# Two of three x blocks as a fourth pair of blocks in an output Strassen scheme, and the same scheme for the first group

## The chip, the cores and the metric

One core of a Trainium2 chip runs the program. The metric is the device time of the program in microseconds (us), the median of several executions; lower is better. Single instructions are looked at in one profiled execution. PE is the matrix engine, PEld its weight loads, DVE the vector engine, ACT the scalar engine, POOL the GpSimd engine, SP the engine whose queue issues nearly all DMAs.

## The reference

A gated linear recurrence (4 batches, 8 heads, 768 steps, head size 48) gives y, which as x of 3072 x 384 enters a feed-forward layer with a maximum over three products:

```python
state = f[:, :, t, :, None] * state + einsum('bhd,bhe->bhde', k[:, :, t], v[:, :, t])
y[:, :, t] = einsum('bhd,bhde->bhe', q[:, :, t], state)
...
h = np.maximum(np.maximum(x @ w1, x @ w2), x @ w3)      # 3072 x 768
return (h @ w_out).astype(np.float32)                    # 3072 x 384
```

All is fp32, the weights are given in fp64 and rounded in the kernel.

## The kernel before

**Algebra.** The kernel forms hm = max(0, x(w2 - w1), x(w3 - w1)) and then out = hm w_out + x (w1 w_out). The 384 x 384 product w1 w_out is computed once, by linear(a) for a = 0, 1, 2 (L724), and kept as w_nat, in the order of features of the first group's x. A copy in the order of features of the later groups' x, w_lin, is made by DMAs (place, L450: ten DMAs a matrix).

**Two kinds of work.** The recurrence runs in 24 rounds u = 0 to 23, each 64 steps of two batches, 128 tokens. Four rounds make a group g of 512 tokens, which then goes through the feed-forward part. In a round the matmuls of the recurrence are pairs (L386), values with sums (L399, L422) and finish (L492); DVE multiplies the result of pairs by a mask (L395) and runs two scans for the next round (scan L324, before L345); POOL multiplies k and q by the scans' results (L340, L351) and the state by its decay (L357); DVE turns kh into ks by sixteen small transposes in four steps (keys_by_blocks, L372), and sums (L436) needs all of them. From round 8 on k, q and f are loaded by blocks and turned on DVE; before that PE transposes them through the PSUM tiles "tr".

**Order.** Everything is issued in an order written by hand (tc.manual_schedule, L927 on), and every engine takes its instructions in that order. The feed-forward part is a generator that yields after each step with an estimate of its PE time (columns x COLUMN, 4 / 2.4 ns). fill(ns) (L902) adds to a budget and takes steps until it is used up. Each round has five fills: before keys, finish and pairs; before after and before of the next round; before values; and two more between the transposes. EARLY (rounds 4 to 7, the last fill 1000 less) and PART (later rounds) are their sizes. What a group has left when the recurrence ends runs alone, with checks of the weights' range (check_range) and, near the end, two small matmuls (L1078, L1079) that read reductions which DVE makes (L1071 to L1075).

**First group** (ffn_first, L738): plain products, then linear, then outputs(hm, xT, i) (L558) for four tiles of 128 tokens, nine matmuls of 384 columns each: six blocks of hm with w_out, three blocks of x with w_nat. Between them POOL makes the mixed weights for the later groups: mix_in (L782) for the inputs, mix (L583) for the outputs, five subtractions of 128 x 576.

**Later groups.** inputs_by_pairs (L807) computes hm by a Strassen scheme over pairs of blocks of x; each of its steps is two matmuls of 256 columns. Three blocks n = 0, 1, 2 of two hm blocks each run interleaved, in the order of L874 to L891. seventh(n) ends with ACT's copy of u3 (L854) and POOL's addition to it (L855); third(n) ends with a DVE addition (L862); fourth(n) ends with two DVE maxima, L869 for the first half of the tokens and L870, which reads u3, for the second, and then sums_of_hm(hm, n) on POOL (L597, four operations of 128 x 256), which forms the sums s1, s2, s4 of the pair and writes one difference in place.

outputs_by_pairs (L599) then computes the 512 tokens by a Strassen scheme of two token tiles, two blocks of a pair and two halves of the columns (HD = 192), p = 0, 1 for the two pairs of tiles. into(b, p, lhs, rhs) (L609) issues three matmuls of 192 columns: over the three pairs of hm blocks for A(k, n), s1, s2, s4, and over the three blocks of x for X(n). A bank is read by ACT into partial (L616) and then written on. The stage opens with X(0) into b for both p, then A(0, 0) into a. sums_of_x(g + 1) (L794) prepares the next group's inputs on POOL near the end of the stage. Results lie in o_four and are stored by store_late in the next group.

Names of places: w_mix[0] is a tile of its own, w_mix[1] to [4] lie in w_in[2]; s_mix lies in w_in[1]; partial is the place of w_nat. Block 3 of a group's xT is free once its rows are packed into the other three, and holds two sums for the inputs.

Of the kernel before, what the change touches and what calls it, by code (L numbers as in the profile page):

```python
# [55 lines left out]
def kernel(  # L56
# [33 lines left out]
    def fast():  # L90
        ctx = ExitStack()
        with ctx:
# [465 lines left out]
            def outputs(hm, xT, i):  # L558
                p = bank()
                t = slice(i % 2 * UT, (i % 2 + 1) * UT)  # L560
                terms = [(hm[:, j, i * UT:(i + 1) * UT], w_out[:, j, :]) for j in range(NJ)]
                terms += [(by_halves(xT)[:, i // 2, k, t], w_nat[:, k, :]) for k in range(NK)]
                for n, (lhsT, rhs) in enumerate(terms):
                    nc.tensor.matmul(p[:, 0:DM], lhsT=lhsT, rhs=rhs, start=(n == 0), stop=(n == NJ + NK - 1))  # L564
                    if n % NK == NK - 1:
                        if n == NJ + NK - 1:
                            o = o_four[:, i]
                            nc.scalar.copy(o, p[:, 0:DM])
                            store(i, o)
                        yield NK * DM * COLUMN  # L570

            HJ, HD = NJ // 2, DM // 2
            corner = lambda k, n: w_out[:, k::2, n * HD:(n + 1) * HD]
            w_mix = [keep.tile([128, HJ, HD], FP32, name="mix")] + [w_in[2][:, :, n * HD:(n + 1) * HD] for n in range(4)]
            s_mix = [w_in[1][:, n, :].rearrange("q (jj t) -> q jj t", jj=HJ) for n in range(NK)]
            partial = [w_in[0][:, n, 0:DM] for n in range(NK)]  # L580
            pairs_of = lambda t: t.rearrange("q (p c) -> q p c", p=2)

            def mix(n):  # L583
# [3 lines left out]
                             (w_mix[4], w_lin[:, :, 0:HD], w_lin[:, :, HD:]))[n]  # L587
                nc.gpsimd.tensor_tensor(dst, x, y, op=ALU.subtract)

            def sums_of_hm(hm, jj):  # L590

                first, second = ([hm[:, 2 * jj + k].rearrange("q (p n t) -> q n p t", p=2, n=2)[:, n] for n in range(2)]
                                 for k in range(2))
                s1, s2, s4 = (pairs_of(t[:, jj]) for t in s_mix)
                for dst, x, y, op in ((s1, first[1], second[1], ALU.add), (s2, s1, first[0], ALU.subtract),
                                      (first[1], first[0], first[1], ALU.subtract), (s4, second[0], s2, ALU.subtract)):
                    nc.gpsimd.tensor_tensor(dst, x, y, op=op)  # L597

            def outputs_by_pairs(g, hm, xT):  # L599
                tile_of = lambda p, n: slice((2 * p + n) * UT, (2 * p + n + 1) * UT)  # L600
                A = lambda k, n: lambda p: hm[:, k::2, tile_of(p, n)]
                X = lambda n: lambda p: xT[:, 0:NK, tile_of(p, n)]
                s1, s2, s4 = (lambda p, t=t: t[:, :, p * UT:(p + 1) * UT] for t in s_mix)
                lin = [w_lin[:, :, n * HD:(n + 1) * HD] for n in range(2)]
# [4 lines left out]
                def into(b, p, lhs, rhs):  # L609
                    for k in range(HJ):  # L610
                        nc.tensor.matmul(b[:, p * HD:(p + 1) * HD], lhsT=lhs(p)[:, k], rhs=rhs[:, k],  # L611
                                         start=id(b) not in begun, stop=(k == HJ - 1), skip_group_check=True)
# [8 lines left out]
                COST = HJ * HD * COLUMN  # L621
                a, b, c = bank(), bank(True), bank(True)
                into(b, 0, X(0), lin[0])
                yield COST
                into(b, 1, X(0), lin[0])
                yield COST
                into(a, 0, A(0, 0), corner(0, 0))
                yield COST
                into(b, 0, A(1, 0), corner(1, 0))
                yield COST  # L630
                into(a, 1, A(0, 0), corner(0, 0))
                read(a, 0)
                yield COST
                into(b, 1, A(1, 0), corner(1, 0))
                add(o_of(0, 0), b, 0)
                yield COST
                into(a, 0, s2, w_mix[1])
                yield COST
                into(a, 1, s2, w_mix[1])
                read(a, 1)  # L640
                yield COST
                into(c, 0, s1, w_mix[0])
                yield COST
                into(c, 1, s1, w_mix[0])
                nc.scalar.copy(tops[:, 2], c[:, 0:DM])
                yield COST
                into(a, 0, A(0, 1), w_mix[2])
# [682 lines left out]
```

## Time and profile before

| | us |
|---|---|
| median of 3 runs (426.74 to 427.01) | 426.76 |
| time of the profiled execution | 427.35 |
| its span, first to last instruction | 425.5 |

Busy time by stretch of that execution (PE's includes modelled ends of pipelined matmuls):

| stretch, us | what runs | PE | DVE | ACT | POOL |
|---|---|---|---|---|---|
| 60 to 70 | first group's products, rounds 4, 5 | 9.39 | 7.97 | 4.24 | 6.05 |
| 70 to 80 | the same, rounds 5, 6 | 9.08 | 6.07 | 7.87 | 3.34 |
| 80 to 90 | linear begins | 9.39 | 6.07 | 7.24 | 6.28 |
| 100 to 110 | first group's outputs | 10.00 | 5.19 | 3.18 | 2.38 |
| 140 to 164 | group 1, inputs | 24.00 | 18.89 | 11.31 | 16.84 |
| 164 to 190 | group 1, outputs | 26.00 | 20.00 | 6.78 | 15.57 |
| 345 to 368 | group 4, outputs, recurrence ends | 23.00 | 1.84 | 9.58 | 7.33 |
| 368 to 397 | group 5, inputs | 29.00 | 5.23 | 19.30 | 12.82 |
| 397 to 425.5 | group 5, outputs, stores | 21.92 | 3.36 | 2.40 | 4.12 |

In a line of the timeline the columns are start, duration (for merged lines, of all of them together), engine, line, operation, output <- inputs, partitions x columns, count; in brackets the idle time of the engine before it and what ended that. "x12" merges twelve records. In the list of waits the columns are the waiting engine and line, what it waited for, us in total, times, longest. A chain's line has start, us and what ran.

### The profile page before, as it was taken

What the parts mean: (1) busy time and instruction counts of PE and PEld (TensorE: products, weight loads), DVE (VectorE), ACT (ScalarE), POOL (GpSimd) and SP (SyncE); (2) the same over time, 40 slices, a digit from 0 to 9 for tenths busy, and PEclk for the clock granted to TensorE, in tenths of its full rate; (3) what the DMA queues carried; (4) which work ended last, traced back from release to release, by engine and by line L of the source; (5) the groups of instructions that cost most, each with busy time, mean ns of one, the idle gap of its engine ahead of it and who ended that gap; (6) DMA issues with size and microseconds to landing.
All of it is one profiled execution on the core that took longest, in us unless ns stands there. A gap on an engine that the chain in (4) does not pass through costs nothing.

```text
span 425.5 us, 11548 instructions
## 1 busy us (share of the span) xinstructions
PE 405.3 (95%) x4650; PEld 340.3 (80%) x4650; DVE 265.4 (62%) x517; ACT 179.9 (42%) x413; POOL 232.8 (55%) x260
## 2 busy tenths in 40 slices
PE   5988799899999999999999999999999999999993
PEld 4766665466567888998889988889988899988993
DVE  6986574952687699868789867888774720012300
ACT  2459566732114442425531444442264424576210
POOL 2178354541888676386586357566546960425600
PEclk9989999999999999999999999999999999999998
DMA  8988987771547753276645276634473011542003
GB/s 170 227 262 259 262 241 119 123 173 51 93 95 119 90 128 54 64 96 103 109 122 109 41 116 81 142 82 87 70 151 86 0 53 42 141 129 66 2 1 78
DMA packets 174617, 47.20 MB, mean 111 GB/s; under 512 B 154016, under 2 KB 172256, under 8 KB 174560
## 3 DMA queue, kind: packets, MB, share of 16 engines
q1 hardware_dynamic: 171216, 45.61, 51.6%
q10 hardware_dynamic: 3344, 0.81, 0.9%
q8 instruction: 37, 0.61, 0.6%
q14 instruction: 20, 0.16, 0.1%
HBM read 37.75 MB, written 4.72 MB: 100 GB/s over the span
## 4 chain that ended last, share of the span: by engine, by line
PE 86%; DVE 3%; SPq 3%; ACT 2%; DMA 2%; issue 1%; POOL 1%; DVEq 0%; POOLq 0%
PE p L819 19%; PE tr L819 16%; PE p L611 14%; PE tr L611 12%; PE p L564 6%; PE p L537 5%; PE p L728 3%; PE y L500 3%; PE y L411 3%; PE a L392 2%; DMA raw<-in_moe_w_dram 2%; SPq L174 2%; PE y L436 2%; PE tr L291 1%; SPq L164 1%
## 5 line engine op out<-in xcount | busy, mean ns | idle before, releaser
L819 PE MATMUL tr<-xT,placed 128*128 128x256 f32 x300 | 73.3, 385 | 0.0
L382 DVE STREAM_TRANSPOSE ks<-kh 32x128 f32<-32x128 f32 x224 | 67.7, 302 | 4.6 <-POOL kh L340 1.0
L819 PEld LDWEIGHTS tr<-xT,placed 128*128 128x128 f32 x300 | 55.6, 190 | 9.1 <-ACT hm L827 1.4
L819 PE MATMUL p<-xT,placed 128*128 128x256 f32 x180 | 45.0, 381 | 0.0
L819 PEld LDWEIGHTS p<-xT,placed 128*128 128x128 f32 x180 | 33.8, 190 | 4.7
L537 PE MATMUL p<-xT,w_in 128*128 128x256 f32 (+1 forms) x108 | 34.3, 458 | 2.9 <-DVE hm L750 2.2
L619 DVE TENSOR_TENSOR o<-tr,w_in 128x384 f32<-128x384 f32 (+1 forms) x11 | 5.7, 514 | 49.6 <-PE tr L611 44.3
L329 DVE TENSOR_TENSOR_SCAN r<-gate,from_one 128x520 f32<-128x520 f32 x24 | 31.3, 1306 | 8.3 <-ACT gate L308 5.3
L340 POOL TENSOR_TENSOR kh<-kt,r 128x512 f32<-128x512 f32 x16 | 28.8, 1798 | 10.6 <-DVE kt L296 10.6
L837 POOL TENSOR_TENSOR hm<-hm,rest_bits 128x512 f32<-128x512 f32 x15 | 22.7, 1512 | 19.1 <-ACT hm L827 19.1
L597 POOL TENSOR_TENSOR w_in<-hm 128x256 f32<-128x256 f32 x15 | 10.9, 727 | 40.5 <-DVE hm L870 40.5
L347 DVE TENSOR_TENSOR_SCAN prod<-gate,from_inv 128x520 f32<-128x520 f32 x24 | 32.5, 1355 | 0.0
L506 ACT COPY xT<-y 64x256 f32<-64x256 f32 (+1 forms) x60 | 22.1, 369 | 24.1 <-PE y L500 23.4
L395 DVE TENSOR_TENSOR at<-a,mask 128x512 f32<-128x512 f32 x24 | 16.5, 688 | 24.2 <-PE a L392 23.9
L258 POOL TENSOR_TENSOR w_in<-top_bits,rest_bits 128x384 uint32<-128x384 uint32 x18 | 21.8, 1211 | 15.5 <-DVE top_bits L254 8.8
L819 PE MATMUL p<-w_in,placed 128*128 128x256 f32 x120 | 30.0, 379 | 0.0
L862 DVE TENSOR_TENSOR hm<-tr,hm 128x512 f32<-128x512 f32 x15 | 10.2, 681 | 29.3 <-PE tr L819 19.3
L537 PEld LDWEIGHTS p<-xT,w_in 128*128 128x128 f32 x108 | 19.3, 190 | 10.7 <-issue 6.2
L655 POOL TENSOR_TENSOR o<-top_bits,w_in 128x384 f32<-128x384 f32 x5 | 5.1, 1015 | 41.6 <-ACT w_in L616 41.6
L616 ACT COPY w_in<-p 128x384 f32<-128x384 f32 x15 | 7.2, 479 | 47.1 <-PE p L611 47.1
L280 ACT ACTIVATE raw<-top_bits 128x384 f32<-128x384 f32 x48 | 25.2, 526 | 0.4
L819 PEld LDWEIGHTS p<-w_in,placed 128*128 128x128 f32 x120 | 22.8, 190 | 3.1
(153 smaller groups left out, 890.5 us busy)
## 6 DMA issues: line engine op xcount, KB each, us to landing
raw<-in_moe_w_dram SPq DMA_DIRECT2D x24, 384.0 KB, 4.2
v_ld<-in_v_dram SPq DMA_DIRECT2D x48, 96.0 KB, 3.2
placed<-in_moe_w_dram SPq DMA_DIRECT2D x12, 384.0 KB, 6.6
out_dram<-o SPq DMA_DIRECT2D x46, 96.0 KB, 2.4
placed<-in_moe_w_out_dram SPq DMA_DIRECT2D x6, 384.0 KB, 6.0
raw<-in_moe_w_out_dram SPq DMA_DIRECT2D x6, 384.0 KB, 3.4
f_ld<-in_f_logit_dram SPq DMA_DIRECT2D x32, 64.0 KB, 2.6
k_ld<-in_k_dram SPq DMA_DIRECT2D x32, 64.0 KB, 2.5
```

Of the source, the lines that this page charges most:

```text
L258: nc.gpsimd.tensor_tensor(dst, by(top), by(rest), op=ALU.add)
L280: nc.scalar.activation(over, size, AF.Relu, scale=(-1 / HI_MIN, 1.0)[step - 1], bias=(1.0, -HI_END * (1 - 2.0 ** -24))[step - 1], accum_ou ...
L329: nc.vector.tensor_tensor_scan(r[:, 0:LEN][:, ::-1], flat(gate)[:, ::-1], flat(from_one)[:, ::-1], 1.0, op0=ALU.mult, op1=ALU.max)
L340: (nc.vector if u < BY_ROWS else nc.gpsimd).tensor_tensor(kh.rearrange("p h a t -> p a h t"), kt, by_batch(r[:, 1:LEN + 1].rearrange("p (x ...
L347: nc.vector.tensor_tensor_scan(flat(prod), flat(gate_tiles[u % 2]), flat(from_inv[u % 2]), 1.0, op0=ALU.mult, op1=ALU.max)
L382: nc.vector.transpose(ks[n * 32:(n + 1) * 32, :, par, e0:e0 + 32], kh[p0:p0 + 32, :, a, t0:t0 + 32])
L506: nc.scalar.copy(xT[o, :, t0 + a * C:t0 + (a + 1) * C], y[i, a, 0:HP * C].rearrange("p (h t) -> p h t", h=HP))
L537: nc.tensor.matmul(p if w < TOK else p.rearrange("p (two t) -> p two t", two=2), lhsT=w_in[i][:, kt, j * 128:(j + 1) * 128], rhs=x[:, t.st ...
L564: nc.tensor.matmul(p[:, 0:DM], lhsT=lhsT, rhs=rhs, start=(n == 0), stop=(n == NJ + NK - 1))
L611: nc.tensor.matmul(b[:, p * HD:(p + 1) * HD], lhsT=lhs(p)[:, k], rhs=rhs[:, k], start=id(b) not in begun, stop=(k == HJ - 1), skip_group_c ...
L819: nc.tensor.matmul(b[:, j * HALF:(j + 1) * HALF], lhsT=w[:, (2 * n + j) * 128:(2 * n + j + 1) * 128], rhs=x, start=begin and j == 0, stop= ...
L837: nc.gpsimd.tensor_tensor(out(n, 0), out(n, 0), first, op=ALU.add)
```

## The change

- In groups 1 to 5 blocks 0 and 1 of x join the output scheme as a fourth pair: into issues four matmuls for A(k, n), s1, s2 and s4, and one (block 2 of x) for X(n). Its sums (sums_of_pair on x) are made on POOL right after those of hm pair 1, its mixed weights (mix_x) once, in group 1, just before them.
- The first group's outputs use outputs_by_pairs too, with three pairs of hm and three plain x blocks. Its sums_of_hm run during linear(1) and linear(2), the five mixes on DVE instead of POOL just before the stage, mix_in inside it, and the copies of w_lin (place) after it. Its stores go through store_late.
- w_mix[0] takes the place of a corner of w_out; partial of group 0 is w_lin, of the others w_nat.
- EARLY goes from 2360 to 2270, PART from 2464 to 2432.

```diff
-            w_mix = [keep.tile([128, HJ, HD], FP32, name="mix")] + [w_in[2][:, :, n * HD:(n + 1) * HD] for n in range(4)]
+            w_mix = [corner(0, 1)] + [w_in[2][:, :, n * HD:(n + 1) * HD] for n in range(4)]
+            x_mix = [w_lin[:, 0, HD:]] + [w_mix[4][:, n] for n in range(2)] + [keep.tile([128, HD], FP32, name="mix")]
+            s_last = keep.tile([128, HALF], FP32, name="s_last")
...
             def mix(n):
...
-                nc.gpsimd.tensor_tensor(dst, x, y, op=ALU.subtract)
+                nc.vector.tensor_tensor(dst, x, y, op=ALU.subtract)
+
+            def mix_x(n):
+                of = lambda k, c: w_lin[:, k, c * HD:(c + 1) * HD]
+                dst, x, y = ((x_mix[2], of(1, 1), of(0, 1)), (x_mix[0], of(0, 1), of(0, 0)),
+                             (x_mix[1], of(1, 1), x_mix[0]), (x_mix[3], of(1, 0), x_mix[1]),
+                             (w_mix[4][:, 2], of(2, 0), of(2, 1)))[n]
+                nc.gpsimd.tensor_tensor(dst, x, y, op=ALU.subtract)
+
+            def sums_of_pair(x0, x1, *sums):
+                first, second = ([x.rearrange("q (p n t) -> q n p t", p=2, n=2)[:, n] for n in range(2)] for x in (x0, x1))
+                s1, s2, s4 = (pairs_of(t) for t in sums)
+                for dst, x, y, op in ((s1, first[1], second[1], ALU.add), (s2, s1, first[0], ALU.subtract),
+                                      (first[1], first[0], first[1], ALU.subtract), (s4, second[0], s2, ALU.subtract)):
+                    nc.gpsimd.tensor_tensor(dst, x, y, op=op)
+
+            def sums_of_hm(hm, jj):
+                sums_of_pair(hm[:, 2 * jj], hm[:, 2 * jj + 1], *(t[:, jj] for t in s_mix))
+
+            def s_of_x(xT):
+                return [xT[:, NK, 0:HALF], xT[:, NK, HALF:TOK], s_last]
...
             def outputs_by_pairs(g, hm, xT):
+                mixed = g > 0
+                A = lambda k, n: lambda p: [hm[:, 2 * jj + k, tile_of(p, n)] for jj in range(HJ)] + [xT[:, k, tile_of(p, n)]] * mixed
+                C = lambda k, n: [w_out[:, 2 * jj + k, half(n)] for jj in range(HJ)] + [w_lin[:, k, half(n)]] * mixed
+                T = lambda i: [w_mix[i][:, jj] for jj in range(HJ)] + [x_mix[i]] * mixed
...
+                if mixed:
+                    X = lambda n: lambda p: [xT[:, 2, tile_of(p, n)]]
+                    partial = [w_nat[:, n, :] for n in range(NK)]
+                else:
+                    X = lambda n: lambda p: [by_halves(xT)[:, p, k, n * UT:(n + 1) * UT] for k in range(NK)]
+                    partial = [w_lin[:, n, :] for n in range(NK)]
...
                 def into(b, p, lhs, rhs):
-                    for k in range(HJ):
+                    for n, (x, w) in enumerate(zip(lhs(p), rhs)):
...
-                COST = HJ * HD * COLUMN
+                COST, PLAIN = (HJ + mixed) * HD * COLUMN, len(lin[0]) * HD * COLUMN
                 a, b, c = bank(), bank(True), bank(True)
                 into(b, 0, X(0), lin[0])
-                yield COST
+                yield PLAIN
                 into(b, 1, X(0), lin[0])
-                yield COST
-                into(a, 0, A(0, 0), corner(0, 0))
+                yield PLAIN
+                into(a, 0, A(0, 0), C(0, 0))
                 yield COST
...
-                    for cost in linear(a):
+                    for n, cost in enumerate(linear(a)):
                         round_to(rounded[0] + 1)
+                        if a and n < 2:
+                            jj = 2 * (a - 1) + n
+                            if jj < HJ:
+                                sums_of_hm(hm, jj)
                         yield cost
+                for n in range(5):
+                    mix(n)
+                for n, cost in enumerate(outputs_by_pairs(0, hm, xT)):
+                    if 3 <= n < 7:
+                        mix_in(n - 3)
+                    yield cost
                 for n in range(2 * NK + 2):
                     place(w_lin, w_nat, n)
-                made = iter([lambda n=n: mix_in(n) for n in range(4)] + [lambda n=n: mix(n) for n in range(5)])
-                for i in range(GRP):
-                    for n, cost in enumerate(outputs(hm, xT, i)):
...
                     sums_of_hm(hm, n)
+                    if n == 1:
+                        if g == 1:
+                            for i in range(5):
+                                mix_x(i)
+                        sums_of_pair(xT[:, 0], xT[:, 1], *s_of_x(xT))
                     yield COST
...
-            EARLY = 2360
-            PART = (33 * TOK + 22 * HJ * HD) * COLUMN / (5 * GRP)
+            EARLY = 2270
+            PART = (33 * TOK + 64 * HD) * COLUMN / (5 * GRP)
```

The other calls of into in outputs_by_pairs stay in their order, with C(k, n) for corner(k, n), T(i) for w_mix[i], lin_mix for w_mix[4], and PLAIN for the X terms.

## Prediction

> **What bounds the kernel now.** I read the busy shares and the forty slices first, then the chain that ended last, then what PE and its weight loads waited for, and last the timeline of each engine around one output stage and around the end.
>
> ```profile
> PE 405.3 (95%) x4650; PEld 340.3 (80%) x4650; DVE 265.4 (62%) x517; ACT 179.9 (42%) x413; POOL 232.8 (55%) x260
> PE   5988799899999999999999999999999999999993
> PE 86%; DVE 3%; SPq 3%; ACT 2%; DMA 2%; issue 1%; POOL 1%; DVEq 0%; POOLq 0%
> ```
>
> PE is full from about 90 us to the end and is 86% of the chain: less PE work shortens the kernel one for one, and every new PE wait lengthens it one for one. In the list of what the weight loads waited for after 160 us, one line concerns the start of the output stage; the timelines of group 1 (PE, DVE, POOL) show where it arises.
>
> ```profile
> PEld p L611 <- DVE hm L869: 0.8, 3, 0.3
> ```
> ```profile
> 163.92 2.11 PE L611 MATMUL tr<-w_in,xT 128*128 128x192 f32 x12
> 165.87 1.39 PE L611 MATMUL p<-w_out,hm 128*128 128x192 f32 x6
> 167.09 1.14 PE L611 MATMUL tr<-w_out,hm 128*128 128x192 f32 x6
> ...
> 168.68 0.63 PE L436 MATMUL y<-v_ld,ks 64*64 64x48 f32 x32
> ```
> ```profile
> 163.19 0.69 DVE L395 TENSOR_TENSOR at<-a,mask 128x512 f32<-128x512 f32 x1
> ...
> 164.54 1.24 DVE L329 TENSOR_TENSOR_SCAN r<-gate,from_one 128x520 f32<-128x520 f32 x1
> ...
> 165.93 0.67 DVE L869 SCALAR_TENSOR_TENSOR hm<-hm,p 128x512 f32<-128x512 f32 x1
> 166.53 0.68 DVE L870 SCALAR_TENSOR_TENSOR hm<-hm,top_bits 128x512 f32<-128x512 f32 x1
> 167.24 1.28 DVE L382 STREAM_TRANSPOSE ks<-kh 32x128 f32<-32x128 f32 x4
> ```
> ```profile
> 159.29 0.73 POOL L597 TENSOR_TENSOR w_in<-hm 128x256 f32<-128x256 f32 x1 [0.63 <-DVE hm L870]
> ...
> 162.15 1.28 POOL L855 TENSOR_TENSOR top_bits<-top_bits,top 128x512 f32<-128x512 f32 x1
> ```
>
> Each fp32 matmul leaves two records (330 calls at L611, 660 records): x12 is six matmuls. The six x-matmuls that open the stage take 165.87 - 163.92 = 1.95 us, **0.325 us a matmul**. The next six records last 1.39 instead of 1.14: their third matmul reads the hm that L869 ends at 166.60, so PE waited 0.25 us. The six x-matmuls are the cover under which DVE, behind the mask and scan of the attention, finishes hm. This wait is there in groups 1, 2 and 3 (3 times, 0.8 us), not in 4 and 5, which have no scan there.
>
> **What the change saves.** A mixed group runs 14 calls of four matmuls and 8 of one, 64 for 66: 5 groups x 2 x 0.325 = 3.25 us. The first group runs 36 matmuls of 384 columns now; the chain has them as
>
> ```profile
> 100.46 1.94 PE p L564 x6
> ...
> 103.89 6.00 PE p L564 x18
> ```
>
> 1.94 / 3 = 0.647 us each, so 23.3 us; after, 66 of 192 columns are 21.45. Saved 1.8. Together **-5.1 us**.
>
> **The opening of the stage, groups 1 to 3.** X(0) is now two matmuls instead of six, while the order of the A terms keeps hm's last pair third. From the budgets and costs the order of emission can be worked out: the last fourth() and X(0) fall in the second fill of u = 11, 15, 19 before and after, so DVE's order (mask, scan, L869) stays. PE therefore comes to the waiting matmul four matmuls, 1.30 us, earlier, and L869 is no earlier: 3 x 1.30 = **+3.9**. Lower bound the same 3.9, since L869 hangs on PE's third(2) through a full DVE; upper the next term.
>
> **POOL's new work in that stretch.** The four sums of x are four more operations of the L597 kind (393.16 to 396.02 in the last group: 2.86 us), queued between the sums of hm pair 1 and the addition L855 of u3. In group 1 five mix_x stand before them: 128x192 by the rows 0.73 (256 columns) and 1.00 (384) is 0.59 each, 3.0 us. Behind L855 hangs L870 on DVE; behind L870 on DVE the transposes L382, the next scan, everything; and PE's L436 needs those transposes. u3 of block 1 is also emitted one fill later, behind kh and qh, so the sums start some 0.6 us later, at 159.9.
> - Group 1: 159.9 + 2.86 + 3.0 + 2.86 + 1.24 = 169.9, with 0.4 for one operation lengthened beside the scan (L597 has 1.67 in such a place) 170.3; L870 to 171.0, L382 to 172.3. PE would be at L436 at 166.97 + 6 x 0.325 + 0.5 = 169.4. Wait **+2.9**, between 1.5 (POOL in step with before, shorter mixes) and 3.6.
> - Groups 2 and 3: without the mixes L855 ends at 167.3, L382 at 169.3, PE needs it at 169.4: **+0.2** for both, 0 to 1.8.
> - The scan L329 now meets POOL at work. Such a scan lasted
>
> ```profile
> 149.67 1.43 DVE L329 TENSOR_TENSOR_SCAN r<-gate,from_one 128x520 f32<-128x520 f32 x1
> ```
>
> against 1.24 with POOL idle: +0.2 before L869 in three groups, **+0.6**, 0 to 0.75. [...]
>
> **The end.** In the last group the same addition of u3 releases L870, L870 the reductions behind it on DVE, and these the two small matmuls L1078 and L1079, which stand in PE's queue inside the output stage.
>
> ```profile
> 396.02 1.28 POOL L855 TENSOR_TENSOR top_bits<-top_bits,top 128x512 f32<-128x512 f32 x1
> ```
> ```profile
> 397.58 0.68 DVE L870 SCALAR_TENSOR_TENSOR hm<-hm,top_bits 128x512 f32<-128x512 f32 x1
> ...
> 398.86 0.15 DVE L1075 TENSOR_SCALAR most<-most 128x1 f32<-128x1 f32 x1
> ```
> ```profile
> 399.69 0.19 PE L1078 MATMUL a<-is_feature,least 128*1 128x1 f32 x2
> ```
>
> With 2.86 of sums in front, L855 ends at 400.16, L870 starts at 400.2, L1075 ends 1.43 later, 401.65. PE, with X(0) of 0.65 and two calls of 1.30 (the fill of 3000 now reaches A(1, 0) too), is there at 396.67 + 3.25 = 399.9: **+1.75**, between 1.2 and 2.2. Today this wait is nil, 399.69 against 399.01.
>
> **Smaller terms.** After X(1) the bank is read by ACT before PE writes it again. ACT's copy ends
>
> ```profile
> 410.89 0.48 ACT L616 COPY w_in<-p 128x384 f32<-128x384 f32 x1 [3.42 <-PE p L611]
> ```
>
> 0.68 us after PE is free (410.69); the cover X(0) lin[1] falls from 1.95 to 0.65, so about 0.15 with the start: five groups **+0.75**, 0.25 to 1.5. In u = 10, 14, 18 L436 comes one step (0.87) earlier than its transposes allow (0.7 of slack: 152.66 to 153.36): 3 x 0.2 = **+0.6**, 0 to 0.9. X(0) of the first group reads w_nat, whose last third ACT ends at 100.98, 0.65 after the stage's start: **+0.15**, 0 to 0.4.
>
> Costed at nothing: the five mixes on DVE, 0.56 for 384 columns (L444) so some 0.8 each. They hide in the 6.9 us for which DVE stands idle before 103.97; contended at 1.5 each they would cost PE 0.3 through the mask. The first group's twelve sums on POOL (8.6 us) sit in its idle time from 91 to 106, behind w_in[1]'s copies, whose last issue ends at 86.86; s2 is read near 108. The copies of w_lin, ten issues of 0.59 us on SP, move behind the first group's outputs, ahead of the f, k, q loads for u = 12 and of v for u = 11, and six stores move behind these; SP stands idle from 154.0 to 162.5, about what the copies (5.9) and the six stores (3.5) take, and v of u = 11, issued near 155, is read at 168. A smaller EARLY moves 1.4 us of matmuls past u = 4 to 6, where PE is idle 2.1 us of 30: taken as 0, -0.7 to +1.4.
>
> **Sum.** -5.1 + 3.9 + 2.9 + 0.2 + 0.6 + 1.75 + 0.75 + 0.6 + 0.15 = **+5.75 us**. The profiled execution has a span of 425.5 and a time of 427.35; it would be 431.2 and 433.1. The median before, 426.76, is 0.6 below that execution's time, so I predict **432.5 us**. All low ends together give +0.9, all high ends +11; not all fall on one side, and the forecast's own range is 429 to 436.
>
> **Rivals.**
> - *The waits are covered* (on the other side, faster). If L869 ended by 165.2 in groups 1 to 3, PE would meet no wait, and with the sums hidden only -5.1 + 0.75 is left: 422.4. For it: DVE is at 62%. Against: its chain from third(2) to L869 (161.2 to 166.6) has no gap over 0.1 us, and it already ends late by 0.25. It decides from L869 before 165.2. 12%.
> - *POOL's additions fit in its idle time.* Then only the opening counts: -5.1 + 3.9 + 0.6 + 0.75 + 0.15 = +0.3, 427.1. For it: POOL is idle 3.9 us before 167.35. Against: that gap lies behind L855, the new work ahead of it. It decides if L855 still ends before 166.5. 16%.
> - *DVE falls behind in every group*: L870 late by 1.5 us in groups 2 and 3 as well and one microsecond more in u = 4 to 6: +9.8, 436.5. For it: POOL operations beside scans lasted 1.67 to 2.0 instead of 0.73 to 1.2. 10%.
> - The change doing less than it says: narrower matmuls bound by weight loads of 190 ns. Against: x12 in 1.95 us is 162 ns a record with such loads. In the rest.
>
> The forecast has 62%. A change of 0.2%, 0.85 us, is what a measurement of this kernel can tell. Below 425.9: the first rival and a little of the second, 0.14. Within: 0.09, the second. Above: 0.77. The range that leaves out no more than a fifth reaches down to the second rival, 426.4, and up to 436.0.
>
> **What would show it.** Right: PE idle of 1.5 us before the third hm matmul of groups 1 to 3, released by L869; L855 of block 2 in group 1 near 170 and PE idle before L436 there; PE idle of 1.7 us before L1078, released by DVE; into() with 772 records (386 matmuls). Wrong: no idle at L611 beyond 0.3, or L1078 without a wait. A PE idle of several us near 100 to 110 would mean that the mixes or the first group's sums were not hidden.

## The result, and the profile after

The changed kernel takes **441.71 us** (median of 4 runs, 438.36 to 442.26) against 426.75: 1.0332 times as long, 95% interval 1.0289 to 1.0376. Slower was right, 432.5 was too low, and the time lies outside the range. The profiled execution took 438.36 us with a span of 436.6 and a mean granted clock of 0.995; the other runs of this measurement had clocks of 0.978 to 0.982 and spans of 439.3 to 440.4.

The busy shares, PE's forty slices and the shares of the chain, in the page of the changed kernel:

```profile
PE 403.6 (92%) x4690; PEld 345.5 (79%) x4690; DVE 273.8 (63%) x524; ACT 180.0 (41%) x414; POOL 256.5 (59%) x293
...
PE   4977898989999995999998999998999999999894
...
PE 77%; DVE 7%; ACT 4%; DMA 3%; POOL 3%; SPq 3%; issue 2%; ACTq 0%; DVEq 0%; POOLq 0%
```

PE is busy 1.7 us less than before and the span is 11.1 longer: PE waits, and its share of the chain falls from 86% to 77%. One slice is down to 5 tenths (about 164 to 175 us, group 1), others in groups 2 and 3 to 8. What PE waited for, from the same profile (engine and line, releaser: us in all, times, longest):

```profile
PE p L619 <- DVE hm L879: 3.5, 2, 1.8
PE y L436 <- DVE ks L382: 3.0, 2, 2.6
...
PE p L736 <- POOL w_out L258: 2.0, 1, 2.0
...
PE p L619 <- DMA f_ld<-in_f_logit_dram: 1.5, 1, 1.5
PE a L1093 <- DVE least L1087: 1.3, 1, 1.3
...
PE p L619 <- ACT w_in L624: 0.6, 1, 0.6
```

(L619 is into of the outputs, L879 and L880 the two maxima of fourth, L865 the addition to u3, L579 mix_x, L587 sums_of_pair, L736 linear, L624 read, L1093 the first small matmul.) The line with f_ld is the opening of group 1: the matmul there reads w_out and hm and no f_ld, and L879 ended its hm at 168.44, 0.05 before PE went on. Each of these waits has its term in the prediction, but for the one at L736.

Cut by the starts of the parts on PE, the kernels of this study look so (us; in the columns after the first two, runs that are told below):

| part | before | after | EARLY 2280 | GpSimd moved, 2270 | both | opening in two passes | s4 ahead | ks ahead | first group alone |
|---|---|---|---|---|---|---|---|---|---|
| linear | 15.92 | 19.84 | 15.92 | 19.83 | 15.92 | 15.93 | 15.92 | 15.92 | 15.92 |
| first group's outputs | 28.72 | 27.14 | 27.15 | 27.14 | 27.14 | 27.14 | 27.15 | 27.15 | 27.41 |
| group 1 | 60.41 | 65.30 | 67.29 | 62.11 | 61.59 | 60.61 | 60.70 | 59.57 | 60.30 |
| group 2 | 60.50 | 62.39 | 61.54 | 61.76 | 61.40 | 60.67 | 60.48 | 59.43 | 60.30 |
| group 3 | 60.51 | 62.36 | 61.54 | 61.78 | 61.40 | 60.67 | 60.48 | 59.43 | 60.30 |
| group 4 | 57.61 | 57.82 | 57.22 | 57.83 | 57.22 | 57.22 | 56.78 | 56.77 | 57.42 |
| group 5, to its last matmul | 51.39 | 52.55 | 52.52 | 50.93 | 50.93 | 50.92 | 49.96 | 49.96 | 51.39 |
| median of the runs | 426.75 | 441.71 | 433.70 | 430.49 | 426.36 | 424.92 | 422.34 | 419.66 | 425.03 |

The part ahead of linear differs by up to 2 us from execution to execution and is left out; in half of the profiles (of these columns before, GpSimd moved and opening in two passes) it holds a stretch of half clock of 3.4 us, at 24 or 45 us. Beside the experiments the kernel before took 427.1 to 427.4; the ratios below are to that.

**Linear, +3.92.** PE's timeline (start, duration, engine, line, operation, output <- inputs; in brackets the idle time before and its releaser), first before, then after:

```profile
89.11 2.75 PE L728 MATMUL p<-w_out,w_in 128*128 128x384 f32 x8
91.70 0.60 PE L291 MATMUL tr<-ident,k_ld 128*128 128x128 f32 x4
```
```profile
87.82 1.13 PE L736 MATMUL p<-w_out,w_in 128*128 128x384 f32 x3
90.92 1.56 PE L736 MATMUL p<-w_out,w_in 128*128 128x384 f32 x2 [1.97 <-POOL w_out L258]
92.27 1.06 PE L291 MATMUL tr<-ident,k_ld 128*128 128x128 f32 x4
```

DVE's timeline around the rounding of the last weight piece (L254), first before, then after:

```profile
85.39 1.05 DVE L254 SCALAR_TENSOR_TENSOR top_bits<-placed,top_bits 128x384 uint32<-128x384 uint32 x1 [0.23 <-issue]
88.79 0.69 DVE L395 TENSOR_TENSOR at<-a,mask 128x512 f32<-128x512 f32 x1 [2.34 <-PE a L392]
90.08 1.24 DVE L329 TENSOR_TENSOR_SCAN r<-gate,from_one 128x520 f32<-128x520 f32 x1 [0.60 <-ACT gate L308]
```
```profile
86.50 0.69 DVE L395 TENSOR_TENSOR at<-a,mask 128x512 f32<-128x512 f32 x1 [2.31 <-PE a L392]
87.81 1.24 DVE L329 TENSOR_TENSOR_SCAN r<-gate,from_one 128x520 f32<-128x520 f32 x1 [0.62 <-ACT gate L308]
...
89.21 0.52 DVE L254 SCALAR_TENSOR_TENSOR top_bits<-placed,top_bits 128x384 uint32<-128x384 uint32 x1
```

The rounding hangs on a step of linear. With EARLY 2270 that step no longer falls into the first fill of round 6, ahead of the mask and the scan, but into the second, behind them; PE waits 1.97 us for it. After the wait, four transposes last 1.06 us instead of 0.60. The windows of 1 us from the same profile say why (busy us and records of PE, PEld, DVE, ACT, POOL, then PE's granted clock, DMA share, GB/s):

```profile
90.00:91.00 1.00, 0.08 (x1) 0.08 (x1) 0.00 (x0) 0.00 (x0) 1.00 (x3) 1.00 0.53 117
91.00:92.00 1.00, 1.00 (x2) 0.56 (x3) 0.00 (x0) 0.00 (x0) 0.92 (x3) 0.52 0.82 209
...
93.00:94.00 1.00, 1.00 (x7) 1.00 (x6) 0.63 (x2) 0.00 (x0) 1.00 (x3) 0.50 0.04 9
94.00:95.00 1.00, 1.00 (x4) 0.64 (x4) 1.00 (x2) 0.00 (x0) 0.92 (x2) 0.77 0.00 0
```

The granted clock is 0.50 for some 3.4 us, which costs 1.7. Such a stretch of half clock is called a dip below.

**Group 1, +4.89.** PE, DVE and POOL at the opening of its outputs:

```profile
165.56 0.81 PE L619 MATMUL tr<-w_in,xT 128*128 128x192 f32 x4
166.21 0.81 PE L619 MATMUL p<-w_out,hm 128*128 128x192 f32 x4
168.49 0.59 PE L619 MATMUL p<-w_out,hm 128*128 128x192 f32 x2 [1.47 <-DMA f_ld<-in_f_logit_dram]
...
174.06 0.31 PE L436 MATMUL y<-v_ld,ks 64*64 64x48 f32 x2 [2.63 <-DVE ks L382]
```
```profile
166.19 1.43 DVE L329 TENSOR_TENSOR_SCAN r<-gate,from_one 128x520 f32<-128x520 f32 x1
...
167.77 0.67 DVE L879 SCALAR_TENSOR_TENSOR hm<-hm,p 128x512 f32<-128x512 f32 x1
172.66 0.69 DVE L880 SCALAR_TENSOR_TENSOR hm<-hm,top_bits 128x512 f32<-128x512 f32 x1 [4.22 <-POOL top_bits L865]
173.38 1.28 DVE L382 STREAM_TRANSPOSE ks<-kh 32x128 f32<-32x128 f32 x4
```
```profile
164.57 1.95 POOL L579 TENSOR_TENSOR w_in<-w_in 128x192 f32<-128x192 f32 x3
...
168.51 2.21 POOL L587 TENSOR_TENSOR xT<-xT 128x256 f32<-128x256 f32 x3
...
171.36 1.26 POOL L865 TENSOR_TENSOR top_bits<-top_bits,top 128x512 f32<-128x512 f32 x1
```

Two x-matmuls instead of six, then PE waits for L879; and L880 stands idle for 4.22 us because POOL works through the differences and sums ahead of L865, so that the transposes behind L880 come late for L436. In group 5 the same delay reaches the small matmuls:

```profile
410.39 0.69 DVE L880 SCALAR_TENSOR_TENSOR hm<-hm,top_bits 128x512 f32<-128x512 f32 x1 [2.53 <-POOL top_bits L865]
```
```profile
411.59 0.19 PE L1093 MATMUL a<-is_feature,least 128*1 128x1 f32 x2 [1.30 <-DVE least L1087]
```

In group 4, 0.60 us of PE's wait is for ACT's read at L624. It is queued there behind the range checks of the weights, the last of which runs from 371.36 to 371.89; the read starts at 371.79.

### The profile page after: what moved, and what is told of

The parts are those of the page before. It is cut to its first block, busy times and chain, and to the rows that moved or that the text cites. A ratio compares the mean times of both kernels' runs of the same rounds, so it can differ in the third digit from the quotient of the medians.

```text
span 436.6 us, 11685 instructions
## 1 busy us (share of the span) xinstructions
PE 403.6 (92%) x4690; PEld 345.5 (79%) x4690; DVE 273.8 (63%) x524; ACT 180.0 (41%) x414; POOL 256.5 (59%) x293
## 4 chain that ended last, share of the span: by engine, by line
PE 77%; DVE 7%; ACT 4%; DMA 3%; POOL 3%; SPq 3%; issue 2%; ACTq 0%; DVEq 0%; POOLq 0%
PE p L829 15%; PE p L619 15%; PE tr L829 15%; PE tr L619 12%; PE p L537 4%; PE y L411 3%; PE p L736 2%; PE y L500 2%; PE y L436 2%; PE a L392 2%; SPq L183 2%; DVE r L329 2%; DMA placed<-w_in 1%; PE tr L291 1%; PE y L407 1%
## 5 line engine op out<-in xcount | busy, mean ns | idle before, releaser
L329 DVE TENSOR_TENSOR_SCAN r<-gate,from_one 128x520 f32<-128x520 f32 x24 | 33.2, 1384 | 9.6 <-ACT gate L308 6.7
L627 DVE TENSOR_TENSOR o<-tr,w_in 128x384 f32<-128x384 f32 (+1 forms) x13 | 6.8, 527 | 51.6 <-PE tr L619 50.3
L624 ACT COPY w_in<-p 128x384 f32<-128x384 f32 x18 | 8.6, 478 | 71.8 <-PE p L619 71.8
L339 POOL COPY ends<-r 128x8 f32<-128x8 f32 x24 | 6.7, 277 | 48.3 <-DVE r L329 48.3
L619 PE MATMUL p<-w_in,hm 128*128 128x192 f32 x144 | 28.8, 336 | 0.6 <-ACT w_in L624 0.6
L587 POOL TENSOR_TENSOR w_in<-hm 128x256 f32<-128x256 f32 x18 | 13.1, 727 | 27.2 <-DVE hm L880 27.2
L619 PE MATMUL tr<-w_out,w_in 128*128 128x192 f32 x144 | 27.1, 327 | 0.5 <-DVE o L627 0.5
L619 PE MATMUL p<-w_in,xT 128*128 128x192 f32 x124 | 26.2, 326 | 0.0
```

The lines of the kernel that those rows point to most:

```text
L329: nc.vector.tensor_tensor_scan(r[:, 0:LEN][:, ::-1], flat(gate)[:, ::-1], flat(from_one)[:, ::-1], 1.0, op0=ALU.mult, op1=ALU.max)
L619: nc.tensor.matmul(b[:, p * HD:(p + 1) * HD], lhsT=x, rhs=w, start=id(b) not in begun, stop=(n == len(rhs) - 1), skip_group_check=True)
```

## The experiments

Theory at the outset: three separate losses, each in its place: the late rounding in linear (with the clock's fall behind it), the thin opening of the outputs, POOL's new work ahead of u3. Rivals: the first group's sums on POOL are what delays linear; the low clocks of the repeated runs have a cause of their own; DVE is simply behind in every group.

### EARLY alone: 2280, and 2360

```diff
-            EARLY = 2270
+            EARLY = 2280
```

> The changed kernel with EARLY 2280 instead of 2270 and nothing else; by the arithmetic of the fills this moves the second linear block (and with it the rounding of weight piece 23) from the second fill of unit 6 back into the first, where the kernel before has it, so that the rounding stands on VectorE ahead of unit 6's mask and unit 7's scan. Theory (the 2.9 us lost ahead of the first group's outputs come from that rounding being late, 2.0 us of wait, and from the lower granted clock that follows the wait): the wait at the second linear block goes, the transposes at 92 us last 0.60 us again, the span falls from 436.6 to about 433.5, and the repeated runs lose their low clocks (0.978 to 0.982) and come to about 435. Rival A (the first group's sums on GpSimd hold up the rounding): wait and span stay as they are. Rival B (the low clock of the repeated runs has another cause): the span falls by about 2, but the repeated runs stay at a clock of 0.98, near 439.

Measured: 433.70 us (433.19 to 434.41), 8.0 less than the changed kernel, for 10 ns in a constant. Linear is back at 15.92, the wait is gone and the transposes last 0.60: the theory, and not the rival on POOL's sums, which are all still there. But the clock did not stay up: in this profile it was 0.50 from 169 to 175.7, behind group 1's wait at L436 (2.07), and group 1 took 67.29 instead of 65.30. Groups 2, 3 and 4 gained as well, 0.85, 0.82 and 0.60, which nobody expected. Their steps are laid out otherwise too: in group 2 single steps of the inputs, two matmuls each, stand one fill earlier, at the opening L880's wait for POOL's addition falls from 0.95 to 0.26, L436 takes 0.63 for 0.95, and PE's wait for L879 is 0.10 shorter. The rest of the 0.85 is not traced. The span fell by 4.9. The clocks of the runs were 0.984 to 0.992.

```diff
-            EARLY = 2270
+            EARLY = 2360
```

> The changed kernel with EARLY as in the kernel before, 2360. The linear stage is laid out as before the change, so by the theory its wait and the clock drop are gone as in the run with 2280, 433 to 434 of span. The difference to 2280 is the phase: groups 0 and 1 are laid out 1.8 us of matrix work earlier against the units' own steps. If phase does not matter, the time is that of the run with 2280 within 0.5 us; if it does, group 1's part changes by a microsecond or more. Rival A (sums on GpSimd): no change from 441.7.

Measured: 442.25 us (441.94 to 442.75), the time that the rival named, but not by its cause: linear lasts 15.93, and groups 1 to 3 took 67.97, 64.86 and 64.86. The phase, how the feed-forward steps lie against the rounds, matters, by far more than a microsecond. PE waited six times at L436 for the ks, 7.1 us in all. The clock fell to 0.50 at 171 to 178, behind a wait of 2.18 at L619, and at 239 to 243 and 304 to 308, behind waits of 2.19 and 2.20 at L436; mean clock 0.977 to 0.979 in all four runs.

### EARLY in the kernel before

```diff
-            EARLY = 2360
+            EARLY = 2270
```

> The kernel before with EARLY 2270 and nothing else: none of the change's sums, differences or blocks. By the arithmetic of the fills the second linear block falls into the second fill of unit 6, as in the changed kernel, and all later groups are laid out one matrix step later. Theory (the linear stage's loss is EARLY's alone): the wait at the second linear block is there, 2.0 us, with the dip of the clock behind it, and the linear stage lasts 19.8 instead of 15.9; the time is 430 to 431, plus what the later groups lose by their phase. Rival (the loss needs the first group's new sums on GpSimd or differences on VectorE): linear stage of 15.9, 427 with the phase's effect.

Measured: 435.79 us (432.66 to 436.09), 1.0202 times the kernel before, interval 1.0172 to 1.0232. The wait is there without any of the change's new work; PE's timeline:

```profile
87.27 2.10 PE L728 MATMUL p<-w_out,w_in 128*128 128x384 f32 x6
91.33 0.91 PE L728 MATMUL p<-w_out,w_in 128*128 128x384 f32 x2 [1.96 <-POOL w_out L258]
92.08 0.60 PE L291 MATMUL tr<-ident,k_ld 128*128 128x128 f32 x4
```

In this execution no dip of the clock followed (transposes 0.60, linear 18.14, mean clock 0.997); the other four runs have 0.985 to 0.989 and are 2.7 to 3.4 us longer. So the wait belongs to EARLY, and the dip behind a wait comes in some executions and not in others. The rest is the phase: 29.88 in the first group's outputs and 61.8 in each of groups 1 to 3, with waits at L869 of 1.35, while group 4 falls to 56.41.

### PE kept busy during the wait

```diff
                         yield cost
+                        if a == 0 and n == 0:
+                            busy(4)
```

> The changed kernel, EARLY 2270, with four matmuls of 256 columns of no use (1.7 us) put on TensorE just ahead of the second linear block, in the place where it waits 2.0 us for the rounding of weight piece 23. The rounding stays as late as it was; only TensorE is busy while it waits. Theory (the drop of the granted clock to 0.50 at 91 us follows from the idle time itself): the transposes behind the wait last 0.60 us instead of 1.06, the linear stage falls from 19.9 to about 18.2, and the runs lie some 1.6 below the changed kernel's, 440 where those are at 441.7. Rival (the drop has another cause, as the load on the chip at that place): transposes of 1.06 and a linear stage of 19.9 or more.

Measured: 438.97 us (438.75 to 439.18); linear 18.15. PE's timeline:

```profile
87.72 1.89 PE L931 MATMUL p<-from_one,ident 128*128 128x256 f32 x8
...
91.78 0.91 PE L736 MATMUL p<-w_out,w_in 128*128 128x384 f32 x2 [0.23 <-POOL w_out L258]
92.53 0.60 PE L291 MATMUL tr<-ident,k_ld 128*128 128x128 f32 x4
```

Useless matmuls of 1.7 us shortened the kernel: the piece comes as late as it did, but the clock holds at 1.00 from 90 to 96 us. One profile without a dip would not show that the idle time is what lets the clock fall, since the wait of 1.96 just above had none either; but all four executions lie within 0.5 us of one another and below all but one of the changed kernel's (438.36 to 442.46 in two measurements). (In this profile the clock fell behind group 1's wait, from 175 to 178.5; group 1 took 66.93.)

### The changed kernel once more

> The changed kernel once more, unaltered, for another profiled execution: its profiled execution took 438.4, the others 441 to 442.3 at a lower mean clock. Theory (a wait of 2 us or more lets the clock fall in some executions and not in others): an execution near 441.7 shows, beside the dip at 91 us, a dip of 6.8 us behind group 1's wait at L436 or behind another wait of more than 1.5 us, each 3.4 us of half clock being worth 1.7. Rival (the slower executions wait longer somewhere): the same dips as in the profile and longer waits or transfers.

Measured: 440.69 us (439.63 to 442.46); the profiled execution took 441.74 at a clock of 0.981. Its waits are those of the first profile to 0.2 us (L436 2.8 and L619 3.5 in all, L736 2.0, L1093 1.3). Its windows around group 1's wait at L436:

```profile
173.00:174.00 1.00, 0.00 (x0) 0.00 (x0) 0.94 (x2) 0.00 (x0) 0.13 (x1) 1.00 0.66 108
174.00:176.00 2.00, 1.36 (x28) 1.20 (x28) 1.91 (x6) 0.00 (x0) 1.92 (x3) 0.61 0.61 196
176.00:178.00 2.00, 2.00 (x8) 1.91 (x8) 2.00 (x3) 0.00 (x0) 2.00 (x4) 0.50 0.00 0
```

Behind the same wait of 2.63, where the first profile shows no dip, half clock until about 181; group 1 took 68.25 instead of 65.30. These 2.95 are nearly all of the 3.3 between the two spans. (Another dip stands at 44 to 48 us, ahead of all that the change touches; linear began 0.4 later.)

### POOL's work moved

```diff
                     sums_of_hm(hm, n)
-                    if n == 1:
-                        if g == 1:
-                            for i in range(5):
-                                mix_x(i)
-                        sums_of_pair(xT[:, 0], xT[:, 1], *s_of_x(xT))
...
                     nc.gpsimd.tensor_tensor(u3, u3, U5[n], op=ALU.add)
+                    if n == NJ // 2 - 1:
+                        sums_of_pair(xT[:, 0], xT[:, 1], *s_of_x(xT))
...
                     join(n)
+                    if g == 1 and n == 1:
+                        for i in range(5):
+                            mix_x(i)
```

> The changed kernel with the five differences of the w_lin blocks on GpSimd moved ahead, to the addition at L847 of step 1 of group 1 (before's GpSimd was idle there for 3.7 us at 143.4), and each group's four sums of x moved behind the addition of u3 of the last step (idle for 3.9 us there). EARLY stays 2270, so the linear stage's loss stays. Theory (in group 1 they delay the addition of u3, and by it L880, the turning of ks and TensorE; in groups 2 and 3 they only stretch the scan): group 1 falls from 65.3 to about 62, groups 2 and 3 by about 0.5 each, group 5 by about 1, together 5 less: 431.5 of span. The waits of TensorE at L436 of 2.6 and at L1093 of 1.3 are gone. Rival (the opening of the outputs, with only two matmuls ahead of the hm blocks, is what costs in all groups): L880 stands no longer behind L865 but the span falls by less than 2.

Measured: 430.49 us (429.44 to 433.30), 11.2 less than the changed kernel, with linear's wait and dip still in it (19.83). Group 1 62.11 as expected, groups 2 and 3 61.8, group 5 50.93, 1.6 less; no wait at L1093, 0.3 at L436. The rival, that only the opening costs, had less than 2. The parts differ by 6.0 from those of the first profile and the medians by 11.2. The profiles stand apart from the medians: the changed kernel's is its fastest execution, 3.4 below its median, and this one lies 2.6 above its own. Without group 1's wait a dip behind it, as the second profile of the changed kernel shows it, has nothing to follow; the clocks, 0.987 to 0.992 in the three slower executions and 0.995 to 0.999 in the four faster, speak for dips as the rest of the difference, but no profile shows it.

With EARLY 2280 as well:

> EARLY 2280 and the GpSimd work of groups 1 to 5 moved (the differences of the w_lin blocks to step 1 of group 1, the sums of x behind the addition of u3). Theory (the two losses are independent and each is paid again by dips of the granted clock to 0.50, of 3.3 to 6.7 us, that follow a wait of 2 us or more): run by run the linear stage lasts 15.9 and group 1 about 61.5, no dip before the end, 427.0 and the runs within 1 us of each other. Rival (each run has its dip somewhere, whichever wait is mended): mean clock 0.985 or less in most runs, 430 or more.

Measured: 426.36 us (425.72 to 427.23, 10 runs), ratio to the kernel before 0.9976 (0.9963 to 0.9989). Clocks 0.991 to 0.997, no dip in the profile from 8 us on until PE is done. So the rival of a dip that finds another place falls: with these waits gone the changed algebra is back at the time of the kernel before.

The differences alone moved, the sums left ahead of u3, EARLY 2280:

> EARLY 2280 and only the five differences of the w_lin blocks moved ahead on GpSimd (step 1 of group 1); the sums of x stay ahead of the addition of u3. Theory (group 1's extra loss is the sum of both: 2.8 of differences and 2.9 of sums, of which the idle 3.9 us ahead of L880 and the slack at L436 take the most; the differences alone are what goes beyond groups 2 and 3): group 1 falls to the time of groups 2 and 3 within 0.5, 61.5 to 62, and the time lies 0.5 to 1.5 above the run in which both were moved, 427 to 428. Rival (the sums of x are what delays u3; the differences fit in idle time): group 1 stays above 63 and the time above 429.

Measured: 429.27 us (428.36 to 429.86); group 1 61.74, groups 2 and 3 61.55 and 61.52, as the theory has it. The time lies 2.9 above the run with both moved instead of 0.5 to 1.5: 1.6 of that is group 5 (52.54 for 50.93), where the sums hold up L880 and the small matmuls; 0.15 each is in groups 1 to 3; what remains is ahead of linear, in the profiled executions 1.1, where this one has a dip at 45 us and the other has none. The differences of w_lin are what made group 1 worse than groups 2 and 3; the sums of x cost at the end.

### The first group's part alone

```diff
-                mixed = g > 0
+                mixed = False
```

with x times w_lin over three blocks in groups 1 to 5 as before, and EARLY 2280.

> The first group's part of the change alone: groups 1 to 5 without the two x blocks inside the scheme (no differences of w_lin blocks, no sums of x; x times the linear weights as three blocks as before, with one difference of w_lin's halves on GpSimd in group 1), PART as before, EARLY 2280 so that the linear stage is laid out as before. Theory (the scheme of the first group saves its 1.6 us and its sums and differences hide): 1.6 below the kernel before, about 425.2, and groups 1 to 5 as before within 0.3 each. Rival (what the first group moves onto GpSimd and VectorE costs it back): 427 or more.

Measured: 425.03 us (423.26 to 425.18), ratio 0.9939 (0.9923 to 0.9956): the first group's outputs save 1.3 (1.6 in the other kernels, a difference that no run explains), and the rest is as before or 0.1 to 0.2 better. The mixes on DVE and the first group's sums on POOL cost nothing that can be seen.

### The opening, the s4 sums and the ks

From the run with both mended, one step after the other. First, the x block ahead in each sum of four, and the three sums that open the stage without their blocks of the third pair (most is every block but the last, rest is the last):

```diff
-                into(a, 0, A(0, 0), C(0, 0))
-                yield COST
-                into(b, 0, A(1, 0), C(1, 0))
-                yield COST
-                into(a, 1, A(0, 0), C(0, 0))
-                read(a, 0)
+                into(a, 0, A(0, 0), C(0, 0), most)
+                yield COST
+                into(a, 1, A(0, 0), C(0, 0), most)
+                into(b, 0, A(1, 0), C(1, 0), most)
+                yield COST
+                into(a, 0, A(0, 0), C(0, 0), rest)
+                into(a, 1, A(0, 0), C(0, 0), rest)
+                read(a, 0)
+                into(b, 0, A(1, 0), C(1, 0), rest)
                 yield COST
```

> As the run with both mended, and the x block stands first in every sum of four blocks, and the outputs open with all blocks that need no hm of the third pair: 2 matmuls of X(0), then 3 each of three sums, 11 matmuls (3.6 us) ahead of the first that waits for L879, where the change left 4 to 6 and the kernel before had 8 (2.6 us). Theory (the fewer covering matmuls cost 1.3 to 1.8 us in each of groups 1 to 3): the waits at L619 behind L879 go, and the time falls by 4 to 5 from the run with both mended, to about 422.5. Rival (VectorE's maxima are late because VectorE itself is behind, so the wait reappears one place later): less than 1.5 gained.

Measured: 424.92 us (424.68 to 425.15), 1.4 less, not 4 to 5: by the median the rival's figure. The waits of 1.5 at L619 are gone, but groups 1 to 3 gain only 0.98, 0.73 and 0.73, together 2.4, and PE waits for ks at L436 instead. (The median shows less than the parts; this profile has a dip at 45 us, ahead of all that the edit touches, and the one before it has none.) Next, with s4's first half ahead of A(1, 1), and fill(8000) ahead of the small matmuls:

```diff
+                into(c, 0, s4, C(1, 1))
+                yield COST
                 into(a, 0, A(1, 1), T(3))
...
-                into(c, 0, s4, C(1, 1))
-                yield COST
                 into(c, 1, s4, C(1, 1))
```

> As the run with the outputs opening in two passes, and the first half of the s4 sums moved ahead of the A(1,1) sums, so that 6 matmuls instead of 2 stand between the last matmul that writes the bank that L624 reads and the next that writes it, and the two small matmuls of the range check come 5 us of matrix work later. Theory: the 0.6 to 0.9 us of wait for that read in group 4 and the wait of 1.3 at the small matmuls go, 1 to 2 below the run before it: about 421, faster than the kernel before by 1.4%. Rival (both waits are hidden by then): the same within 0.5.

Measured: 422.34 us (422.09 to 424.00), 2.6 less, ratio 0.9896 (0.9865 to 0.9927); group 4 gains 0.44, group 5 0.96. Another 1.0 between the profiles is ahead of linear, where the dip at 45 us is not in this one; that is not the edit's. What is left in groups 1 to 3 stands in DVE's and PE's timelines of group 2 (here the two maxima are L885 and L886):

```profile
224.22 0.67 DVE L885 SCALAR_TENSOR_TENSOR hm<-hm,p 128x512 f32<-128x512 f32 x1
224.81 1.01 DVE L886 SCALAR_TENSOR_TENSOR hm<-hm,top_bits 128x512 f32<-128x512 f32 x1
225.84 1.28 DVE L382 STREAM_TRANSPOSE ks<-kh 32x128 f32<-32x128 f32 x4
```
```profile
226.15 0.69 PE L436 MATMUL y<-v_ld,ks 64*64 64x48 f32 x6
227.18 0.66 PE L436 MATMUL y<-v_ld,ks 64*64 64x48 f32 x26 [0.34 <-DVE ks L382]
227.77 0.92 PE L619 MATMUL p<-w_out,hm 128*128 128x192 f32 x4
```

L436 takes from 226.15 to 227.77, 1.62 us, where without a wait it takes 0.57. So the last four transposes of ks were put ahead of the fill that holds the third maxima:

```diff
-                    fill(part)
                     keys_by_blocks(u, 3)
+                    fill(part)
```

> As the run with the s4 sums and the small matmuls moved, and on VectorE the transposes that fill the last fourth of ks (L382) are issued ahead of the second fill of each unit, no longer behind it, so that the third pair's maxima, which that fill holds in units 11, 15 and 19, no longer stand ahead of them. Theory (with the opening covered, what is left of the loss in groups 1 to 3 is VectorE's queue: mask, gate, scan, two maxima, ks, one behind the other, 0.65 us of shorter TensorE work and some 0.5 us of slower scan and maxima beside GpSimd; the ks come last and TensorE waits at L436): the wait at L436 goes, groups 1 to 3 fall from 60.5 or 60.7 to about 59.6, and the time falls by 2.5 to 3, to 419.5. Rival (the wait goes over to the third pair's maxima, now 1.3 later, or to the next unit's kt and scan): less than 1 gained.

Measured: **419.66 us** (418.39 to 420.63, 5 runs), ratio to the kernel before 0.9827 (0.9803 to 0.9851), the fastest of all. DVE and PE in the same place:

```profile
222.49 1.28 DVE L382 STREAM_TRANSPOSE ks<-kh 32x128 f32<-32x128 f32 x4
223.80 0.69 DVE L885 SCALAR_TENSOR_TENSOR hm<-hm,p 128x512 f32<-128x512 f32 x1
224.41 0.68 DVE L886 SCALAR_TENSOR_TENSOR hm<-hm,top_bits 128x512 f32<-128x512 f32 x1
```
```profile
224.32 0.63 PE L436 MATMUL y<-v_ld,ks 64*64 64x48 f32 x32
```

Groups 1 to 3 fall by 1.13, 1.05 and 1.05, and no wait of PE is left there. The maxima now end 0.8 us after L436 begins (225.09), instead of 0.3 before it, and PE does not wait for them: the two passes cover them.

## Why the prediction was wrong, step by step

- **The step that failed: "A smaller EARLY ... taken as 0, -0.7 to +1.4".** It counted idle PE time and did not ask what else hangs on a step of linear. The rounding of the last weight piece does, and it went behind the mask and the scan on DVE: 1.97 of wait and 1.7 of half clock, 3.92 in linear; by the same constant groups 2 to 4 lie 2.3 worse in phase than with 2280 (0.85 + 0.82 + 0.60). In the medians, dips included, it is worth 8.0, and the kernel before, given the same constant, loses 8.4. With 2280 in its place the change takes 433.7, 1.2 above the forecast; that this is so near is in part luck, since its profile has a dip of 6.8 us behind group 1's wait that no term held. To leave EARLY at 2360 would have cost as much, 442.25, by waits in groups 1 to 3: what the step took as nothing is how every later step falls against the rounds.
- **A term that was missing: the clock.** No step allowed for PE's waits lowering its granted clock. In the first profile it cost 1.7, in the second another 3.4 of clock behind group 1's wait, 2.95 of time; the other executions have no profile, only mean clocks of 0.978 to 0.990, where the first has 0.995 and the second 0.981.
- **-5.1 saved:** right. First group 1.58 for 1.65 (1.8 less the 0.15 of the w_nat term); a mixed group 0.65, two matmuls, read between the last two kernels' group 4 (57.42 for the first group alone, 56.77 with the mixed blocks and no wait), which differ in the order of s4 and ks too.
- **+3.9 for the opening:** mechanism, place and releaser right; waits of 1.47, 1.76 and 1.75 where 0.25 stood and 1.55 was expected. Its whole price, with the scan's term in it, is 61.40 with POOL mended against 60.30 - 0.65 = 59.65 (group 2 with the first group's part alone, less two matmuls): 1.75 a group, 5.3 for three, where 1.30 and 0.2 a group were expected, 4.5 for three. 0.73 a group is cured by cover and 1.05 by the order of the ks on DVE: the cover alone moves the wait to L436. There the rival that DVE falls behind was half right.
- **+2.9 for group 1's POOL:** right: group 1 is 2.91 longer than group 2 in the changed kernel. The wait at L436 is 2.63. L865 ended at 172.6 and not at 170.3, but PE came to L436 as much later, near 171.4 and not at 169.4, 1.4 of it because all of group 1 began later.
- **+0.6 for the scan beside POOL:** right in kind, too small: the scans of groups 1, 2 and 3 at the openings lasted 1.43, 1.71 and 1.71 for 1.24, together 1.13 more, where 0 to 0.75 was allowed.
- **+1.75 at the end:** right; 1.61 between the runs with the sums ahead of and behind u3 (52.54 and 50.93).
- **+0.75 for the read after X(1):** a wait of 0.60 in one group, the fourth, with ACT's range checks ahead of the read, where five of 0.15 were expected; 0.2 of it is left with EARLY 2280.
- **+0.6 for L436 at u = 10, 14, 18:** right; the 32 records of L436 take 0.86, 0.87 and 0.87 there for 0.63. **+0.2 for groups 2 and 3:** 0.32 in each (0.95 for 0.63), 0.64, inside its range. The low ends of the terms add up to +1.05, not +0.9; nothing rests on it.
- **The rivals:** L869 (now L879) ended at 168.4 in group 1, not before 165.2, and L855 (now L865) at 172.6, not before 166.5, so the first two fell. A record of 192 columns lasts 326 ns at the median before and after, so narrower matmuls were not the cause either.
- **Costed at nothing:** for the mixes on DVE, the first group's sums and SP's copies this held: the first group's outputs took 27.14, and PE has no wait for them there.

## What to carry to other kernels

A constant that only sizes the slices of an interleaved schedule moves whole steps past one another; whoever changes one should list, for each step that moves, every instruction that hangs on it on the other engines, and try the neighbouring values, since 10 ns were worth 8 us here. When a change saves matmuls that cover another engine's work, look one wait further: filling the first hole moved the wait to the next result of the same queue, and only both together gave the saving. Where PE is full, a wait may not be the whole price: here waits of 2.0 to 2.6 us were followed, in some executions, by another 1.7 or 3.4 us of lost clock.

## What was not expected of the hardware

Behind waits of about 2 us PE's granted clock fell to 0.50, for 3.4 or 6.8 us. Lost clock, summed over the windows: 0.48 + 0.50 + 0.50 + 0.23 = 1.71 us at 91 us, which is 3.4 us at one half; in the second execution 0.78 + 2.00 + 0.64 = 3.42 in group 1 (174 to 182), 6.8 us, twice as long. It followed waits of 1.97 in two executions of the changed kernel and of 1.96 in the run with POOL's work moved, and not the same wait of 1.96 in the kernel before with EARLY 2270; the wait of 2.63 in one execution of the changed kernel and not in the other.

How the wait falls in time decides it, as far as these profiles show. In each of them the changes of the clock lie on a grid with steps of 3.41 us, and each dip before the last matmul lasts one or two steps. Cut by that grid, the fourteen profiles have, from 60 us to the last matmul, nine steps at full clock in which PE's timeline is busy for 0.46 of the time or less, and a dip follows each; none follows a step with 0.48 or more. The wait of 1.97 lay whole in one step (87.6 to 91.0, busy 0.42); the 1.96 without a dip was cut in two (0.57 and 0.85). The wait of 2.63 was cut in two in the first profile (0.55 and 0.58) and lay in one step in the second (0.23). Ahead of 60 us the share alone does not decide: dips follow steps of 0.53 to 0.61 at 42 us, and none follows steps of 0.46 to 0.55 at 28 us. Why some dips last two steps stays open.
